# Gating on ScalarE, x sums moved, two sums reordered, and a rearranged last pair in a fused attention and mixture-of-experts kernel

## The chip, the cores and the metric

The kernel runs on one core of a Trainium2 chip. The time is the device time of that core in microseconds (us). A program on one core has no second die to compare with, so a run counts as fast unless it is over 1.5% above the fastest of its kernel.

Short names of the engines: PE is TensorE (matrix products), DVE is VectorE, ACT is ScalarE, POOL is GpSimd, SP is SyncE (here it issues stores). PEld is the loading of TensorE's stationary operand. PSUM is the memory that TensorE writes its products to (the tiles named `ps`), SBUF the memory that holds the other tiles. A name with a q, such as SPq, is an engine's own issue queue.

## The reference, cut to what matters

```python
x = cosformer_attention(q, k, v)          # 4608 tokens x 512; scaled, kept transposed
logits = x @ w_gate                       # 4608 x 8 experts
P = np.exp(logits - logits.max())
for _ in range(8):                        # the routing: rows and columns in turn
    P /= P.sum(1, keepdims=True) + 1e-09
    P /= P.sum(0, keepdims=True) + 1e-09
    P *= N / E
for e in range(8):
    h = np.maximum(x @ w1[e], 0.0)
    out += P[:, e:e + 1] * (h @ w2[e])
```

Every expert runs over all tokens. The output is a sum over experts, each part scaled per token by its column of `P`; this scaling is called the gating.

Of the kernel before, what the change touches and what calls it, by code (L numbers as in the profile page):

```python
# [25 lines left out]
def kernel(  # L26
# [10 lines left out]
    nc = tc.nc  # L37
# [12 lines left out]
    FT = F // P  # L50
    TCH = 512
    NJ = N // TCH
    assert KT == HK and N % TCH == 0

    ctx.enter_context(nc.allow_low_precision("fp16 operands of the matmuls"))
    ctx.enter_context(nc.allow_non_contiguous_dma(reason="256 byte runs and up"))
# [103 lines left out]
            else:  # L160
                ve.tensor_copy(out=acc(g), in_=y_ps)

    def store(g, both=False):
        for half in range(2):
            w_ = 2 * g + half
            b, c = w_ // C, w_ % C
            rows = out[b * S : (b + 1) * S].rearrange("(p c) d -> p c d", c=C)
            (nc.scalar if half and both else nc.sync).dma_start(
                out=rows[:, c, :], in_=acc(g)[half * HP : (half + 1) * HP, :]
            )  # L170

    with ExitStack() as p1:
# [413 lines left out]
                    fn(*args)  # L586


    se = nc.scalar
    ps_k = ctx.enter_context(tc.tile_pool(name="ps_k", bufs=1, space=bass.MemoryType.PSUM))  # L590
    wB = ctx.enter_context(tc.tile_pool(name="wB", bufs=1))
    hB = ctx.enter_context(tc.tile_pool(name="hB", bufs=1))
# [103 lines left out]

    def snapshot(ps, name):
        t = u_pool.tile([P, TU], F16, name=name)
        nc.scalar.copy(out=t[:], in_=ps[:, 0:TU])
        return t  # L700

    late = []
# [1 line left out]
    def group(hT, tw, xs, n, i, fill):  # L704

        b11, T1, b21, b22, T2, T3, T4 = tw
        s1, s2, s4 = (t[:] for t in xs)
        h11, h12 = hT[:, i, 0:TU], hT[:, FH + i, 0:TU]
        h21, h22 = hT[:, i, TU : 2 * TU], hT[:, FH + i, TU : 2 * TU]
        X = ps_h[0].tile([P, TCH], FP32, name="h_ps")  # L710
        product(X, b11, x_part(0, 0, n), True)
        nc.scalar.copy(out=Y[:, 0:TU], in_=X[:, 0:TU])  # L712
        fill()
        for fn in late:
            fn()
        late.clear()
        fill()
        product(X, T2, s2, False)
        u2 = snapshot(X, "u2")
        fill()  # L720
        product(Y, b21, x_part(0, 1, n), False)
        nc.scalar.activation(out=h11, in_=Y[:, 0:TU], func=AF.Relu)  # L722
        fill()
        product(X, T1, s1, False)
        u4 = snapshot(X, "u4")
        fill()
        product(Z, T3, x_part(1, 0, n), True)
        add_relu(h22, Z, u4)
        fill()
        product(X, b22, s4, False)  # L730
        nc.scalar.activation(out=h12, in_=X[:, 0:TU], func=AF.Relu)  # L731
        fill()

        def last():
            product(Z, T4, x_part(1, 1, n), False)
            add_relu(h21, Z, u2)

        late.append(last)


    class Pair:
        def __init__(self, k, hT, e, w, c1, g1, c2, g2, first, last):
            self.last = last
            self.hT, self.e, self.w, self.g1, self.g2, self.first = hT, e, w, g1, g2, first
            self.a11, self.a12 = hT[:, 0:FH, c1 : c1 + P], hT[:, FH:FT, c1 : c1 + P]
            self.a21, self.a22 = hT[:, 0:FH, c2 : c2 + P], hT[:, FH:FT, c2 : c2 + P]
            self.rows = rows2[k % 3][:]
            self.U, self.V = self.rows[:, 0:DH], self.rows[:, DH : 2 * DH]
            self.W = W2[:, k % 2 * DH : (k % 2 + 1) * DH]

        def mult(self, ps, lhs, rhs, start=False):
# [4 lines left out]
                )  # L756

        def add(self, g, rows, a=None):
            a = acc(g) if a is None else a
            ve.scalar_tensor_tensor(  # L760
                out=a, in0=rows, scalar=P_tok[:, g, self.e : self.e + 1], in1=a,
                op0=ALU.mult, op1=ALU.add,
            )

        def sums(self):
            name = "hs_last" if self.last else "hs"
            pool = u_pool if self.last else hs_pool
            S1, S2, S4 = (pool.tile([P, FH, P], F16, name=f"{name}{k_}") for k_ in (1, 2, 4))
            for out_, in0, in1, op in (
                (S1[:], self.a21, self.a22, ALU.add), (S2[:], S1[:], self.a11, ALU.subtract),  # L770
                (self.a21, self.a11, self.a21, ALU.subtract),
                (S4[:], self.a12, S2[:], ALU.subtract),
            ):
                (nc.gpsimd if self.last else ve).tensor_tensor(  # L774
                    out=out_, in0=in0, in1=in1, op=op
                )
            self.S1, self.S2, self.S4 = S1[:], S2[:], S4[:]

        def step(self, name):
# [3 lines left out]
            if name == "P1":  # L783
                if self.first:

                    tw2[0:2] = [t_pool.tile([P, FH, DH], F16, name=f"V{k_}")[:] for k_ in (2, 3)]
                    ve.tensor_tensor(out=tw2[0], in0=b22, in1=b12, op=ALU.subtract)
                    ve.tensor_tensor(out=tw2[1], in0=tw2[0], in1=b11, op=ALU.subtract)
                self.mult(self.U, self.a11, b11, True)
                nc.scalar.copy(out=self.W, in_=self.U)  # L790
                if not self.last:
                    self.sums()
            elif name == "P7":

                if self.first:
                    tw2[2:3] = [t_pool.tile([P, FH, DH], F16, name="V4")[:]]
                    ve.tensor_tensor(out=tw2[2], in0=b21, in1=tw2[0], op=ALU.subtract)
                self.mult(self.V, self.a21, tw2[1])
            elif name == "P6":
                self.mult(self.U, self.S2, tw2[0])  # L800
                self.add(self.g2, self.rows)
            elif name == "P2":
                self.mult(self.W, self.a12, b21)
                self.add(self.g1, self.W, acc(self.g1)[:, 0:DH])
            elif name == "P4":
                self.mult(self.V, self.a22, tw2[2])
                if self.last:
                    self.add(self.g2, self.V, acc(self.g2)[:, 0:DH])
                    store(self.g2, True)
            elif name == "P5":  # L810
                self.mult(self.U, self.S1, b12)
                if self.last:
                    self.add(self.g2, self.U, acc(self.g2)[:, DH:Dm])
                    return
                swapped = self.rows.rearrange("p (h d) -> p h d", h=2)[:, ::-1, :]
                self.add(self.g2, swapped, acc(self.g2).rearrange("p (h d) -> p h d", h=2))
                if self.e == E - 1:
                    store(self.g2)
            elif name == "P3":
                self.mult(self.U, self.S4, b22)  # L820
                self.add(self.g1, self.U, acc(self.g1)[:, DH:Dm])
                if self.e == E - 1:
                    store(self.g1, self.last)

    tw2 = [None] * 3

    def w2_first(w):
        b11, b12 = w[1][:, 0:FH, 0:DH], w[1][:, 0:FH, DH:Dm]
# [65 lines left out]

        return [(n * UG + i, NG // 2 + n * UG + i) for i in range(UG)]

    def gate(n):

        for pair in of_unit(n):
            for g in pair[::-1]:  # L900
                nc.gpsimd.tensor_scalar(  # L901
                    out=acc(g), in0=acc(g), scalar1=P_tok[:, g, 0:1], scalar2=None, op0=ALU.mult,
                )


    balance = sinkhorn()
# [2 lines left out]
    for i in range(FH):  # L909
        tw, tw_steps[3 + i] = w1_steps(w_next, i)  # L910
        tws.append(tw)
    xs_next = x_tiles()
    sums_x = x_sums(0, xs_next)
    for j in range(B - 1, NJ):
        hT = next_h()
        tiles = halves(hT, w0, [(ts * P, j * TCH // P + ts) for ts in range(TCH // P)])
        for slot in range(NS):
# [7 lines left out]
                gates(B - 1, Z[:])  # L925
            if j == B - 1 and slot:
                next(sums_x, None)
            since = (j - B + 1) * NS + slot - 5
            if since == -4:
                balanced(3)  # L930
# [3 lines left out]

    OFFSETS = {"P1": 0, "P2": 3, "P7": 4, "P6": 5, "P4": 8, "P5": 9, "P3": 13}

    OFFSETS_LAST = {"P1": 0, "P7": 4, "P6": 5, "P2": 7, "P5": 8, "P4": 9, "P3": 10}
    stream = []
    slot2 = -2
    n_pairs = 0  # L940

    def add_pairs(hT, e, w, n):
        nonlocal n_pairs
        for i, (g1, g2) in enumerate(of_unit(n)):
            last = e == E - 1 and n == NU - 1 and i == UG - 1
            pair = Pair(n_pairs, hT, e, w, i * P, g1, TU + i * P, g2, n == 0 and i == 0, last)
            for name, offset in (OFFSETS_LAST if last else OFFSETS).items():
                stream.append((7 * n_pairs + offset, pair, name))
            n_pairs += 1
# [13 lines left out]
    def pair_fill():  # L963
        nonlocal k_fill, slot2
        k_fill += 1
        if k_fill % 4 and stream and stream[0][0] <= slot2:
            _, pair, name = stream.pop(0)
            pair.step(name)
        slot2 += bool(k_fill % 4)

    mark(Y[:])
    for e in range(1, E):
        w = w_next
        for n in range(NU):
            hT = next_h()
            xs = xs_next
            for i in range(FH):
                group(hT, tws[i], xs, n, i, start_fill if e == 1 and n == 0 else pair_fill)
                m = (n + 1) % NU
                if e == 1 and m:  # L980

                    if i == 0:
                        xs_next = x_tiles()
                        sums_x = x_sums(m, xs_next)
# [15 lines left out]
            if e == 1 and n == 0:  # L1000
# [4 lines left out]
                    pass  # L1005
                mark(W2[:])
                w2_first(w)
                ve = nc.vector
            if e == 1:
                gate(n)  # L1010
            if n == 0 and e + 1 < E:
                w_next = new_weights(wA if e % 2 else wB)
                load_w1(w_next, e + 1, 1)
# [2 lines left out]
            add_pairs(hT, e, w, n)  # L1016
    for fn in late:
        fn()

    stream[-1][1].sums()  # L1020
    while stream:
        _, pair, name = stream.pop(0)
        pair.step(name)
# [1 line left out]
_INS = ['q', 'k', 'v', 'moe_w_gate', 'moe_w1', 'moe_w2']  # L1025
_OUTS = [((4608, 512), 'float32')]
# [25 lines left out]
```

## The kernel before: the parts that the change touches

Expert 0 is computed plainly while the attention and the routing still run, so its part goes into the accumulator `acc` before `P` is known. It has to be multiplied by `P[:, 0]` later; this is the gating that the change moves. There are 36 tiles `acc(g)` of 128 tokens by 512 columns in fp32.

Experts 1 to 7 use a Strassen-like scheme of seven products in place of eight, which needs sums of blocks of x, of the weights and of h. The tokens of an expert are cut into six units. A unit has four groups of seven products for `h` (each product is two matmuls of 384 columns), and between them stand the steps of "pairs": a pair is two tiles of 128 tokens, with seven products P1 to P7 of four matmuls of 256 columns.

Three engines serve TensorE. In each group ScalarE copies or takes the relu out of PSUM five times. VectorE makes the other relus in one custom instruction that adds a snapshot ("add-and-relu", 0.54 to 0.56 us each in the trace before), makes four sums of halves of h for each pair, and adds the gated products into `acc`.

```python
def group(hT, tw, xs, n, i, fill):        # fill() emits the next step of a pair
    X = ps_h[0].tile([P, TCH], FP32, name="h_ps")
    product(X, b11, x_part(0, 0, n), True)
    nc.scalar.copy(out=Y[:, 0:TU], in_=X[:, 0:TU])     # one such copy per group
    fill()
    # ... the last product of the group before, into Z ...
    fill()
    product(X, T2, s2, False)
    u2 = snapshot(X, "u2")                # the first snapshot, on ScalarE
    fill()
    product(Y, b21, x_part(0, 1, n), False)
    nc.scalar.activation(out=h11, in_=Y[:, 0:TU], func=AF.Relu)
    fill()
    product(X, T1, s1, False)
    u4 = snapshot(X, "u4")                # the second snapshot
    fill()
    product(Z, T3, x_part(1, 0, n), True)
    add_relu(h22, Z, u4)                  # VectorE; frees the bank Z
    fill()
    product(X, b22, s4, False)
    nc.scalar.activation(out=h12, in_=X[:, 0:TU], func=AF.Relu)
    fill()

def sums(self):                           # of one pair; a21 is overwritten by a11 - a21
    # ...
    for out_, in0, in1, op in (
        (S1[:], self.a21, self.a22, ALU.add), (S2[:], S1[:], self.a11, ALU.subtract),
        (self.a21, self.a11, self.a21, ALU.subtract),
        (S4[:], self.a12, S2[:], ALU.subtract),
    ):
        (nc.gpsimd if self.last else ve).tensor_tensor(out=out_, in0=in0, in1=in1, op=op)

def gate(n):                              # in the second expert, once per unit n
    for pair in of_unit(n):
        for g in pair[::-1]:
            nc.gpsimd.tensor_scalar(
                out=acc(g), in0=acc(g), scalar1=P_tok[:, g, 0:1], scalar2=None, op0=ALU.mult,
            )
# ...
stream[-1][1].sums()                      # the last pair's sums, on GpSimd
while stream:                             # the steps of the last pairs, without groups between
    _, pair, name = stream.pop(0)
    pair.step(name)
```

TensorE's instructions are held in written order to the end. ScalarE's are in the attention part, and VectorE's up to the second expert's first unit; after that a scheduler orders them, and may move one ahead of another where nothing depends on the order.

The softmax here doesn't subtract the row's maximum and nothing guards it: scores larger than these inputs give would overflow.

## Time and profile before

The time is 1012.0 us (median of four runs, 1011.84 to 1012.25).

| what | reading | view |
|---|---|---|
| TensorE busy | 983.8 us, 97% of the span | page, part 1 |
| TensorE idle, 200 to 300 us | 6.7 us | windows of 5 us |
| of it waits on VectorE's add-and-relu | 3.5 us in five waits | timeline of TensorE |
| GpSimd's gatings | 36, on average 1.66 and 1.68 us in the two groups | groups by form |
| half rate in the tail | four groups, 0.99 to 1.06 us instead of 0.60 us | timeline |

These lines of the page give the busy time of the engines and, for TensorE, VectorE and GpSimd, the share of each of 40 equal slices in tenths (9 is 90% and more).

```profile
PE 983.8 (97%) x8062; PEld 690.7 (68%) x8062; DVE 840.3 (83%) x1861; ACT 556.5 (55%) x1250; POOL 117.3 (12%) x116
PE   7999999998999999999999999999999999999996
DVE  5888777689999888888879888988789888987876
POOL 6312200009930000000000000000000000000001
```

TensorE is at 9 in every slice but the first, the last and the tenth. In the tenth and eleventh GpSimd is at 9, and VectorE is at 9 as well (56.3 of the 60 us from 228 to 288 us).

The timeline of TensorE between 215 and 280 us, the lines with a mark of idle time (start, duration, engine, line, operation, and in brackets the idle time before it and what ended it):

```profile
219.66 0.20 PE L100 MATMUL copied_ps<-colp,ones_col 128*1 128x8 f32 x2 [1.20 <-DVE colp L100]
224.84 0.20 PE L100 MATMUL copied_ps<-colp,ones_col 128*1 128x8 f32 x2 [0.78 <-DVE colp L100]
...
235.97 0.48 PE L100 MATMUL p_ps<-xT,T_0_3375 128*128 128x384 f16 x2 [0.77 <-DVE H L693]
246.50 0.48 PE L100 MATMUL p_ps<-xT,T_2_3381 128*128 128x384 f16 x2 [1.14 <-DVE H L693]
256.34 0.48 PE L100 MATMUL p_ps<-xT,T_0_3375 128*128 128x384 f16 x2 [0.74 <-DVE H L693]
...
275.79 0.48 PE L100 MATMUL p_ps<-xT,T_0_3375 128*128 128x384 f16 x2 [0.53 <-DVE H L693]
```

The first two waits are for the routing's column sums (`colp`). The others are for the add-and-relu (line 693), which must empty the bank `p_ps` (called Z in the code) before the next product into it.

Why VectorE is late shows in the groups by form between 228 and 288 us (line, engine, operation, shapes, count, then busy us and the mean of one in ns). The first line is GpSimd's gating; the next are VectorE's sums of two fp16 tiles in SBUF, and the last an add that reads PSUM.

```profile
L901 POOL TENSOR_SCALAR acc_lo<-acc_lo,P_tok 128x512 f32<-128x512 f32 x32 | 53.2, 1678 | 16.7 <-DVE P_tok L100 16.6
L774 DVE TENSOR_TENSOR H<-H 128x512 f16<-128x512 f16 x9 | 4.8, 529 | 0.0
L774 DVE TENSOR_TENSOR hs_4203<-hs_4202,H 128x512 f16<-128x512 f16 x1 | 1.2, 1190 | 0.0
L760 DVE SCALAR_TENSOR_TENSOR acc_lo<-rows_ps,P_tok,acc_lo 128x512 f32<-128x512 f32 x16 | 11.8, 740 | 2.6 <-PE rows_ps L100 2.6
```

A sum takes up to 1.19 us there, and 0.42 us between 340 and 400 us, where GpSimd is quiet. The add that reads PSUM takes 0.74 us there and 0.75 us later. So the sums are slow beside GpSimd's gatings and the add that reads PSUM is not; below, such a slowing is called a collision. But not every sum is hit: GpSimd is busy for 59.4 of the 60 us, and 11 of the 36 sums take 0.57 us or more, while 25 keep 0.41 to 0.44 us. What decides which sums are hit is not shown.

The tail, in the timeline, with the same columns:

```profile
989.77 1.21 POOL L774 TENSOR_TENSOR hs_last_13227<-hs_last_13226,H 128x512 f16<-128x512 f16 x1
990.00 1.26 DVE L774 TENSOR_TENSOR hs_13251<-hs_13250,H 128x512 f16<-128x512 f16 x1
991.18 1.37 DVE L774 TENSOR_TENSOR H<-H 128x512 f16<-128x512 f16 x1
...
992.60 0.61 PE L100 MATMUL rows_ps<-V_12078,H 128*128 128x256 f16 x4 [1.98 <-DVE H L774]
...
994.55 0.99 PE L100 MATMUL rows_ps<-w2e,hs_13178 128*128 128x256 f16 x4 [0.90 <-DVE acc_hi L760]
995.34 1.06 PE L100 MATMUL rows_ps<-w2e,H 128*128 128x256 f16 x4
```

GpSimd's sums for the last pair collide with VectorE's for an earlier pair: those of VectorE take up to 1.37 us, and those of GpSimd rise from 1.15 to 1.33 us. TensorE waits 1.98 us for the third of these, `a11 - a21` (written into `H`), then 0.90 us more, and then its matmuls run at about half the rate for a while: four groups last 0.79 to 0.86 us from start to start, where 0.44 us is usual. The granted clock is 0.70 from 995 to 1000 us, 0.96 in the 5 us before and 1.00 from 985 to 990 us.

### The profile page before, as it was taken

How to read it: one execution, taken by the hardware profiler on the slowest of the kernel's cores; microseconds unless marked ns; L12 is line 12 of the kernel's file. 1: busy time of each engine (PE TensorE's matmuls, PEld its weight loads, DVE VectorE, ACT ScalarE, POOL GpSimd, SP SyncE). 2: the span in 40 equal slices, each digit the busy share in tenths (PEclk: the TensorE clock that was granted, in tenths of full speed). 3: DMA queues.
4: the chain of work that ended last, by engine and by line, in shares of the span. 5: the costliest groups of instructions: out<-in, count | busy, mean ns of one | idle time of the engine just before them, and what ended most of it. 6: DMA issues, size and time to landing. Idle time of an engine off the chain costs nothing.

```text
span 1010.2 us, 20651 instructions
## 1 busy us (share of the span) xinstructions
PE 983.8 (97%) x8062; PEld 690.7 (68%) x8062; DVE 840.3 (83%) x1861; ACT 556.5 (55%) x1250; POOL 117.3 (12%) x116
## 2 busy tenths in 40 slices
PE   7999999998999999999999999999999999999996
PEld 6555555445677777777777777777777777777775
DVE  5888777689999888888879888988789888987876
ACT  5766666355555555555555555555555555555551
POOL 6312200009930000000000000000000000000001
PEclk8999999999999999999999999999999999999998
DMA  9966510531302331044013310133103401114434
GB/s 168 201 91 86 88 20 1 107 58 41 81 24 50 64 67 47 25 80 76 25 48 66 65 49 25 36 78 66 49 24 67 89 25 33 39 33 127 113 87 113
DMA packets 51762, 66.50 MB, mean 66 GB/s; under 512 B 4816, under 2 KB 43472, under 8 KB 51664
## 3 DMA queue, kind: packets, MB, share of 16 engines
q0 software_dynamic: 27232, 30.94, 19.8%
q1 hardware_dynamic: 24272, 33.98, 12.4%
q8 instruction: 63, 1.03, 0.4%
q14 instruction: 35, 0.29, 0.1%
q10 hardware_dynamic: 160, 0.26, 0.1%
HBM read 83.12 MB, written 12.98 MB: 95 GB/s over the span
## 4 chain that ended last, share of the span: by engine, by line
PE 88%; DVE 9%; DMA 1%; issue 1%; ACT 1%; POOL 0%; DVEq 0%; POOLq 0%; ACTq 0%
PE rows_ps L100 32%; PE h_ps L100 25%; PE p_ps L100 10%; PE copied_ps L100 10%; PE y_ps L100 5%; PE small_ps L100 4%; DVE H L693 1%; DVE k_p L100 1%; DVE acc_lo L760 1%; DMA k_ld<-in_k_dram 1%; DVE q_pT L100 1%; DVE acc_hi L760 1%; DVE q_p L100 0%; DMA q_ld<-in_q_dram 0%; DVE den L100 0%
## 5 line engine op out<-in xcount | busy, mean ns | idle before, releaser
L760 DVE SCALAR_TENSOR_TENSOR acc_lo<-rows_ps,P_tok,acc_lo 128x512 f32<-128x512 f32 (+1 forms) x322 | 205.0, 640 | 75.1 <-PE rows_ps L100 75.1
L100 PEld LDWEIGHTS <-H 128*128 128x128 f16 x2080 | 203.5, 98 | 85.6 <-DVE H L774 2.3
L100 PEld LDWEIGHTS <-w1e 128*128 128x128 f16 x1632 | 155.8, 98 | 58.3 <-issue 3.6
L100 PE MATMUL h_ps<-xT,w1e 128*128 128x384 f16 (+1 forms) x616 | 152.9, 350 | 0.0
L731 ACT ACTIVATE H<-h_ps 128x384 f16<-128x384 f32 x168 | 82.5, 491 | 112.0 <-PE h_ps L100 112.0
L712 ACT COPY copied_ps<-h_ps 128x384 f32<-128x384 f32 x168 | 78.7, 468 | 41.2 <-PE h_ps L100 40.3
L722 ACT ACTIVATE H<-copied_ps 128x384 f16<-128x384 f32 x168 | 82.7, 492 | 23.5 <-PE copied_ps L100 23.5
L100 PE MATMUL rows_ps<-w2e,H 128*128 128x256 f16 (+1 forms) x568 | 91.7, 286 | 0.0
L100 PE MATMUL copied_ps<-xT,w1e 128*128 128x384 f16 x336 | 82.1, 326 | 0.0
L100 PE MATMUL copied_ps<-w2e,H 128*128 128x256 f16 x504 | 75.6, 273 | 0.0
L118 POOL DMA_DIRECT2D w1e<-in_moe_w_dram x11 | 8.3, 770 | 455.2 <-DVE T_3_10517 L671 83.4
L760 DVE SCALAR_TENSOR_TENSOR acc_lo<-copied_ps,P_tok,acc_lo 128x256 f32<-128x256 f32 x126 | 60.1, 477 | 0.5
L760 DVE SCALAR_TENSOR_TENSOR acc_hi<-rows_ps,P_tok,acc_hi 128x512 f32<-128x512 f32 (+1 forms) x57 | 42.0, 736 | 20.5 <-PE rows_ps L100 20.3
L790 ACT COPY copied_ps<-rows_ps 128x256 f32<-128x256 f32 x126 | 45.0, 357 | 23.3 <-PE rows_ps L100 23.0
L901 POOL TENSOR_SCALAR acc_lo<-acc_lo,P_tok 128x512 f32<-128x512 f32 x32 | 53.2, 1678 | 16.7 <-DVE P_tok L100 16.6
L100 PE MATMUL y_ps<-w2e,hT 128*128 128x512 f16 x224 | 54.7, 380 | 0.0
L774 DVE TENSOR_TENSOR H<-H 128x512 f16<-128x512 f16 x125 | 54.1, 433 | 0.0
L100 ACT ACTIVATE hT<-h_ps 128x512 f16<-128x512 f32 x54 | 32.3, 600 | 17.0 <-PE h_ps L100 16.6
L100 DVE TENSOR_TENSOR xT<-small_ps,rb 128x384 f16<-128x384 f32 x64 | 26.2, 451 | 16.6 <-ACT rb L100 16.5
L100 PEld LDWEIGHTS <-hT 128*128 128x128 f16 x224 | 19.5, 98 | 25.0 <-issue 5.8
L100 ACT COPY rb<-small_ps 128x384 f32<-128x384 f32 x64 | 22.4, 402 | 22.7 <-PE small_ps L100 22.6
L100 DVE TENSOR_SCALAR q_pT<-small_ps 128x384 f16<-128x384 f32 x46 | 25.0, 553 | 9.3 <-PE small_ps L100 8.8
(2450 smaller groups left out, 2036.3 us busy)
## 6 DMA issues: line engine op xcount, KB each, us to landing
out_dram<-acc_lo SPq DMA_DIRECT2D x63, 128.0 KB, 2.4
w1e<-in_moe_w_dram POOLq DMA_DIRECT2D x7, 1024.0 KB, 9.0
w2e<-in_moe_w_dram POOLq DMA_DIRECT2D x7, 1024.0 KB, 9.3
k_ld<-in_k_dram POOLq DMA_DIRECT2D x16, 288.0 KB, 6.3
v_ld<-in_v_dram POOLq DMA_DIRECT2D x16, 288.0 KB, 6.9
q_ld<-in_q_dram POOLq DMA_DIRECT2D x16, 288.0 KB, 6.4
w1e<-in_moe_w_dram POOLq DMA_DIRECT2D x4, 256.0 KB, 10.5
w2e<-in_moe_w_dram POOLq DMA_DIRECT2D x4, 256.0 KB, 10.8
```

What stands on the lines that cost most here:

```text
L100: i = getattr(self.engine, name)(*args, **kwargs)
L118: nc.gpsimd.dma_start(out=w[0][:, :, f0:f1], in_=view[:, :, f0:f1])
L693: latest = ve._custom_dve(TENSOR_ADD_SAT, out=out, in0=ps[:, 0:TU], in1=t[:], s0=FP32_MAX, s1=0.0)
L712: nc.scalar.copy(out=Y[:, 0:TU], in_=X[:, 0:TU])
L722: nc.scalar.activation(out=h11, in_=Y[:, 0:TU], func=AF.Relu)
L731: nc.scalar.activation(out=h12, in_=X[:, 0:TU], func=AF.Relu)
L760: ve.scalar_tensor_tensor(out=a, in0=rows, scalar=P_tok[:, g, self.e : self.e + 1], in1=a, op0=ALU.mult, op1=ALU.add,)
L774: (nc.gpsimd if self.last else ve).tensor_tensor(out=out_, in0=in0, in1=in1, op=op)
L790: nc.scalar.copy(out=self.W, in_=self.U)
L901: nc.gpsimd.tensor_scalar(out=acc(g), in0=acc(g), scalar1=P_tok[:, g, 0:1], scalar2=None, op0=ALU.mult,)
```

## The change

Its intent: take the gating from GpSimd, so that VectorE is not held up, and give it to ScalarE, which is 55% busy; take four sums of x out of the second expert's first unit; and shorten the tail. The diff, cut to its core:

```diff
-            if e == 1:
-                gate(n)                                   # six tiles at once, on GpSimd
+def gate(g, pool=None):
+    if pool is None:
+        se.mul(out=acc(g), in_=acc(g), mul=P_tok[:, g, 0:1])          # ScalarE
+    else: ...                                             # GpSimd, for the first two tiles only
 def pair_fill():
     ...
+        if (k_fill % 7 == 6 or k_fill % 7 == 4 and k_fill % 4 in (1, 2)) and ungated:
+            gate(ungated.pop(0))
+        if e == 2:
+            se = nc.scalar           # ScalarE in written order to the end of the second expert
 # x sums of the second unit, beside the last plain block of expert 0
+            if j == NJ - 1:
+                if slot == 0:
+                    sums_x = x_sums(1, xs_first[1])
+                next(sums_x, None)
 def sums(self, after=None):
-                (S1[:], self.a21, self.a22, ALU.add), (S2[:], S1[:], self.a11, ALU.subtract),
+                (S1[:], self.a21, self.a22, ALU.add),
                 (self.a21, self.a11, self.a21, ALU.subtract),
+                (S2[:], S1[:], self.a11, ALU.subtract),
                 (S4[:], self.a12, S2[:], ALU.subtract),
+                # the last pair's (GpSimd) wait for `after`, VectorE's last sum of the pair before
-    OFFSETS_LAST = {"P1": 0, "P7": 4, "P6": 5, "P2": 7, "P5": 8, "P4": 9, "P3": 10}
+    OFFSETS_LAST = {"P1": 0, "P2": 3, "P7": 4, "P6": 7, "P5": 8, "P4": 9, "P3": 10}
+            if last:
+                self.V = Z[:, 0:DH]                       # the two halves in two banks
 # the last tile is stored in two column halves, the first as soon as P2 is in
+                    store(self.g1, slice(0, DH), both)    # both = (nc.sync, nc.scalar)
+                        store(self.g1, slice(DH, Dm), both)
-    stream[-1][1].sums()
     while stream:
         _, pair, name = stream.pop(0)
         pair.step(name)
+        if pair is final[-2] and name == "P1":
+            final[-1].sums(pair.summed)
```

The second and third of the four sums change places. (`k_fill` counts the calls of `fill()`, and so sets at which steps a gating is emitted.)

More of the change, by code (lines that the diff above doesn't have):

```diff
@@ L52 @@
     NJ = N // TCH
-    assert KT == HK and N % TCH == 0
+    assert NG % 12 == 0 and KT == HK and N % TCH == 0
     ctx.enter_context(nc.allow_low_precision("fp16 operands of the matmuls"))
@@ L161, in ffn2, with store @@
                 ve.tensor_copy(out=acc(g), in_=y_ps)
-    def store(g, both=False):
-        for half in range(2):
+    def store(g, cols=slice(0, Dm), queues=(nc.sync, nc.sync)):
+        for half, queue in enumerate(queues):
             w_ = 2 * g + half
@@ L167, in store @@
             rows = out[b * S : (b + 1) * S].rearrange("(p c) d -> p c d", c=C)
-            (nc.scalar if half and both else nc.sync).dma_start(
-                out=rows[:, c, :], in_=acc(g)[half * HP : (half + 1) * HP, :]
+            queue.dma_start(
+                out=rows[:, c, cols], in_=acc(g)[half * HP : (half + 1) * HP, cols]
             )
@@ L586 @@
                     fn(*args)
-    se = nc.scalar
     ps_k = ctx.enter_context(tc.tile_pool(name="ps_k", bufs=1, space=bass.MemoryType.PSUM))
@@ L698, in snapshot @@
         t = u_pool.tile([P, TU], F16, name=name)
-        nc.scalar.copy(out=t[:], in_=ps[:, 0:TU])
+        se.copy(out=t[:], in_=ps[:, 0:TU])
         return t
@@ L711, in group @@
         product(X, b11, x_part(0, 0, n), True)
-        nc.scalar.copy(out=Y[:, 0:TU], in_=X[:, 0:TU])
+        se.copy(out=Y[:, 0:TU], in_=X[:, 0:TU])
         fill()
@@ L721, in group @@
         product(Y, b21, x_part(0, 1, n), False)
-        nc.scalar.activation(out=h11, in_=Y[:, 0:TU], func=AF.Relu)
+        se.activation(out=h11, in_=Y[:, 0:TU], func=AF.Relu)
         fill()
@@ L730, in group @@
         product(X, b22, s4, False)
-        nc.scalar.activation(out=h12, in_=X[:, 0:TU], func=AF.Relu)
+        se.activation(out=h12, in_=X[:, 0:TU], func=AF.Relu)
         fill()
@@ L758, in add @@
         def add(self, g, rows, a=None):
+            assert g not in ungated
             a = acc(g) if a is None else a
@@ L763, in add, with sums @@
             )
-        def sums(self):
+        def sums(self, after=None):
             name = "hs_last" if self.last else "hs"
@@ L769, in sums @@
             for out_, in0, in1, op in (
-                (S1[:], self.a21, self.a22, ALU.add), (S2[:], S1[:], self.a11, ALU.subtract),
+                (S1[:], self.a21, self.a22, ALU.add),
                 (self.a21, self.a11, self.a21, ALU.subtract),
+                (S2[:], S1[:], self.a11, ALU.subtract),
                 (S4[:], self.a12, S2[:], ALU.subtract),
             ):
-                (nc.gpsimd if self.last else ve).tensor_tensor(
+                i = (nc.gpsimd if self.last else ve).tensor_tensor(
                     out=out_, in0=in0, in1=in1, op=op
                 )
+                if self.last and after is not None:
+                    tc.add_manual_dep(
+                        i.ins,
+                        after.ins.name,
+                        mybir.DependencyInfo(
+                            mybir.DependencyClass.Sync, mybir.DependencyReason.DATA
+                        ),
+                        reason="VectorE's sums first",
+                    )
+                    after = None
+            self.summed = i
             self.S1, self.S2, self.S4 = S1[:], S2[:], S4[:]
@@ L789, in step @@
                 self.mult(self.U, self.a11, b11, True)
-                nc.scalar.copy(out=self.W, in_=self.U)
+                se.copy(out=self.W, in_=self.U)
                 if not self.last:
@@ L797, in step @@
                     ve.tensor_tensor(out=tw2[2], in0=b21, in1=tw2[0], op=ALU.subtract)
-                self.mult(self.V, self.a21, tw2[1])
+                self.mult(self.V, self.a21, tw2[1], self.last)
             elif name == "P6":
                 self.mult(self.U, self.S2, tw2[0])
-                self.add(self.g2, self.rows)
+                if self.last:
+                    self.add(self.g2, self.U, acc(self.g2)[:, 0:DH])
+                    self.add(self.g2, self.V, acc(self.g2)[:, DH:Dm])
+                else:
+                    self.add(self.g2, self.rows)
             elif name == "P2":
@@ L804, in step @@
                 self.add(self.g1, self.W, acc(self.g1)[:, 0:DH])
+                if self.last:
+                    store(self.g1, slice(0, DH), both)
             elif name == "P4":
@@ L808, in step @@
                     self.add(self.g2, self.V, acc(self.g2)[:, 0:DH])
-                    store(self.g2, True)
+                    store(self.g2, queues=both)
             elif name == "P5":
@@ L822, in step @@
                 if self.e == E - 1:
-                    store(self.g1, self.last)
+                    if self.last:
+                        store(self.g1, slice(DH, Dm), both)
+                    else:
+                        store(self.g1)
     tw2 = [None] * 3
+    both = (nc.sync, nc.scalar)
     def w2_first(w):
@@ L895, in of_unit @@
         return [(n * UG + i, NG // 2 + n * UG + i) for i in range(UG)]
-    def gate(n):
-        for pair in of_unit(n):
-            for g in pair[::-1]:
-                nc.gpsimd.tensor_scalar(
-                    out=acc(g), in0=acc(g), scalar1=P_tok[:, g, 0:1], scalar2=None, op0=ALU.mult,
-                )
+    def gate(g, pool=None):
+        if pool is None:
+            se.mul(out=acc(g), in_=acc(g), mul=P_tok[:, g, 0:1])
+        else:
+            pool.tensor_scalar(
+                out=acc(g), in0=acc(g), scalar1=P_tok[:, g, 0:1], scalar2=None, op0=ALU.mult,
+            )
+    ungated = [g for n in range(NU) for pair in of_unit(n) for g in pair]
     balance = sinkhorn()
@@ L911 @@
         tws.append(tw)
-    xs_next = x_tiles()
+    xs_first = [x_tiles() for _ in range(2)]
+    xs_next = xs_first[0]
     sums_x = x_sums(0, xs_next)
@@ L935 @@
     OFFSETS = {"P1": 0, "P2": 3, "P7": 4, "P6": 5, "P4": 8, "P5": 9, "P3": 13}
-    OFFSETS_LAST = {"P1": 0, "P7": 4, "P6": 5, "P2": 7, "P5": 8, "P4": 9, "P3": 10}
+    OFFSETS_LAST = {"P1": 0, "P2": 3, "P7": 4, "P6": 7, "P5": 8, "P4": 9, "P3": 10}
     stream = []
+    final = []
     slot2 = -2
@@ L946, in add_pairs @@
             pair = Pair(n_pairs, hT, e, w, i * P, g1, TU + i * P, g2, n == 0 and i == 0, last)
+            if e == E - 1 and n == NU - 1:
+                final.append(pair)
             for name, offset in (OFFSETS_LAST if last else OFFSETS).items():
@@ L980 @@
                 if e == 1 and m:
+                    if n == 0:
+                        xs_next = xs_first[1]
+                        continue
                     if i == 0:
@@ L1007 @@
                 w2_first(w)
+                for _ in range(2):
+                    gate(ungated.pop(0), nc.gpsimd)
                 ve = nc.vector
-            if e == 1:
-                gate(n)
             if n == 0 and e + 1 < E:
```

## The prediction

The gains of 2.9, 3.8 and 0.4 us come to 7.1 us, which takes 1012.0 us to 1004.9, given as 1005.0 us.

> **What bounds the kernel.** TensorE: busy 97%, and 88% of the chain that ended last. So the change can win back only TensorE's idle or slow time. By windows of 5 us, TensorE idles 6.7 us between 200 and 300 us, almost never from 300 to 980.
>
> The 6.7 us, from the idle marks of the timeline: 2.0 us waiting for the routing's column sums on VectorE (219.7 and 224.8 us); 1.2 us on ScalarE copies (213 to 234 us); 3.5 us in five waits on VectorE's add-and-relu (236 to 276 us). There GpSimd runs 36 gatings, 1.66 us each (226 to 288 us), and VectorE is 100% busy. Its fp16 additions (128x512) take 0.8 to 1.2 us when they collide, against 0.42 us later. [...] the adds that read PSUM keep 0.74 us.
>
> In the tail GpSimd's four sums (988.5 to 993.6 us) collide with another pair's sums on VectorE (up to 1.37 us instead of 0.42). TensorE idles 2.0 + 0.9 us, then runs four groups at half rate (1.06 instead of 0.60 us). After 990.46 us, 20 steps of 0.437 us could end at 999.4; they end at 1006.0.
>
> **What changes.** TensorE's order changes only in the last pair.
> - 34 gatings move to ScalarE, an estimated 0.70 us each (from a 128x512 activation's 0.60 us and a 128x576 one from SBUF, 0.67), 24 us in all; ScalarE, 55% busy, rises to about 80%. Most fit the idle 0.66 us before the relu that waits for TensorE. Those before the second snapshot have only 0.2 to 0.3 us: 1 to 2 us of stall in all. The scheduler hoists the last four to about 232 us, where two stand before a snapshot: 1 to 1.5 us of stall.
> - Four x sums (0.55 us each) move from 215–231 us to VectorE's gaps near 201–206 us: most of the 2.0 us returns.
> - VectorE's 3.5 us of waits nearly vanish: without GpSimd it needs about 96% of TensorE's time.
>
> Middle: idle falls from 6.7 to about 3.8 us. Gain 2.9 us.
> - Tail: GpSimd starts after VectorE's sums, whose four take 1.6 us instead of 4.4, and the half rate should go. But VectorE's remaining work (11.4 us) is longer than TensorE's 9, and GpSimd's chain of four (about 1 us each, from 995.5) may hold the last pair 0.5 to 1 us. Two banks remove one of two waits of 0.57 us. Gain about 3.8 us. The last store is half as large: 0.4 us.
>
> **Prediction: 1005.0 us, range 1001.5 to 1008.5.** Faster by over 2%: 1%; within 2%: 98%; slower: 1%.
>
> **What would show it.** Fp16 sums at 0.42 us and no TensorE wait on add-and-relu from 240 to 290 us; gatings of 0.70 us on ScalarE; TensorE waits on snapshots of 2 to 3 us between 230 and 320 us; sums from 989 to 997 us at 0.42 us; no half-rate matmuls; a wait for GpSimd's last sums.
>
> **What would make it wrong.** Gatings delay snapshots more, so that stalls only change owner (1008); the tail still idles over 2 us before the last pair [...] (1007); or the gatings fit everywhere and the tail is nearly gapless (1001).

## The result, and the profile after

The kernel after takes 1003.08 us (median of four runs, 1002.52 to 1004.44), the kernel before 1012.01 us. The ratio of the fast runs is 0.9914, with an interval of 0.9896 to 0.9931: within 2%, and 8.9 us faster. A ratio is the mean time of one kernel's fast runs over that of the other's of the same rounds, so it is not quite the ratio of the medians.

The page of the kernel after, the busy time:

```profile
PE 981.3 (98%) x8062; PEld 689.3 (69%) x8062; DVE 829.2 (83%) x1862; ACT 574.7 (57%) x1284; POOL 60.3 (6%) x82
```

The timeline of TensorE shows only these marks over 0.3 us between 215 and 300 us:

```profile
219.13 0.19 PE L100 MATMUL copied_ps<-colp,ones_col 128*1 128x8 f32 x2 [1.20 <-DVE colp L100]
224.31 0.20 PE L100 MATMUL copied_ps<-colp,ones_col 128*1 128x8 f32 x2 [0.78 <-DVE colp L100]
```

All five waits on the add-and-relu are gone, and both waits on the column sums are there to the hundredth. The groups by form, VectorE's sums between 228 and 288 us, and ScalarE's gatings:

```profile
L777 DVE TENSOR_TENSOR H<-H 128x512 f16<-128x512 f16 x9 | 3.8, 419 | 0.1
L100 ACT ACTIVATE acc_lo<-acc_lo,P_tok 128x512 f32<-128x512 f32 x28 | 20.4, 727 | 0.0
```

The sums are back at 0.42 us. A gating takes 0.73 us, 4% more than the 0.70 us that the prediction estimated from two ScalarE activations in the trace before (128x512 in 0.60 us, and 128x576 from SBUF in 0.67 us).

The tail, in the timeline:

```profile
984.11 0.43 DVE L777 TENSOR_TENSOR H<-H 128x512 f16<-128x512 f16 x1
984.45 0.42 DVE L777 TENSOR_TENSOR hs_13244<-hs_13243,H 128x512 f16<-128x512 f16 x1
...
991.95 0.33 PEld L100 LDWEIGHTS <-H 128*128 128x128 f16 x4 [0.23 <-POOL H L777]
993.06 0.33 PEld L100 LDWEIGHTS <-hs_last_13295 128*128 128x128 f16 x4 [0.34 <-POOL hs_last_13295 L777]
994.25 0.60 PE L100 MATMUL rows_ps<-w2e,hs_last_13294 128*128 128x256 f16 x4 [0.58 <-DVE acc_hi L762]
```

VectorE's sums take 0.42 us, and no group of matmuls runs at half rate. Two weight loads wait for GpSimd's chain of sums, by 0.23 and 0.34 us. The first load of a group usually starts 0.10 us ahead of its products (988.61 and 988.71 us) and here 0.01 us (991.95 and 991.96 us), so the two groups of products start later by less: 0.55 and 0.66 us after the group before, where 0.44 us is usual.

### Where the time came from

TensorE's order of instructions is the same in both kernels up to the last pair, so the same instruction can be looked up in both and the times compared. ScalarE's copy of X to Y is a handy landmark: there is one in each of the 168 groups. The first, the 30th (in the third expert's second unit) and the 168th, from the timeline of ScalarE, before:

```profile
209.60 0.46 ACT L712 COPY copied_ps<-h_ps 128x384 f32<-128x384 f32 x1
349.40 0.46 ACT L712 COPY copied_ps<-h_ps 128x384 f32<-128x384 f32 x1 [0.33 <-PE h_ps L100]
983.33 0.46 ACT L712 COPY copied_ps<-h_ps 128x384 f32<-128x384 f32 x1 [0.33 <-PE h_ps L100]
```

and after:

```profile
209.07 0.46 ACT L100 COPY copied_ps<-h_ps 128x384 f32<-128x384 f32 x1
345.85 0.46 ACT L711 COPY copied_ps<-h_ps 128x384 f32<-128x384 f32 x1 [0.33 <-PE h_ps L100]
977.59 0.46 ACT L711 COPY copied_ps<-h_ps 128x384 f32<-128x384 f32 x1 [0.33 <-PE h_ps L100]
```

They cut the span into pieces: the start (to the first copy), the middle (first to 30th), the steady part (30th to 168th), the tail (to the start of the last four matmuls, from the timeline), and the end (to the end of the span). The two spans are 1010.2 and 1000.8 us.

| piece | before | after | gain |
|---|---|---|---|
| start | 209.60 | 209.07 | 0.53 |
| middle | 139.80 | 136.78 | 3.02 |
| steady | 633.93 | 631.74 | 2.19 |
| tail | 22.04 | 17.84 | 4.20 |
| end | 4.83 | 5.37 | -0.54 |

The start varies from 208.33 to 211.20 us over the twelve profiles (the kernels before and after and ten variants), and the end from 4.47 to 5.37 us, with no pattern that follows an edit. So these two pieces are read as noise, and they are most of the scatter of the times. The middle and the tail repeat to about 0.1 us where an edit doesn't touch them, the steady part to 0.3 us (see below). These three pieces are what the experiments are judged by.

The gain of 2.19 us in the steady part was in no term of the prediction. By the spacing of the landmarks it lies in six steps of 0.33 us, one near the start of each expert from the third on, and in one of 0.28 us at the 109th group. The latter, a gap without a mark in TensorE's products, is absent from every variant with the gating on ScalarE and present in the two that keep it on GpSimd; why is not known. The timeline at the first of the six, before:

```profile
348.62 0.42 DVE L774 TENSOR_TENSOR hs_5236<-H,hs_5235 128x512 f16<-128x512 f16 x1
348.95 0.55 DVE L693 CUSTOM_DVE_ANT_0 H<-p_ps,u_5246 128x384 f16<-128x384 f32 x1
...
349.56 0.48 PE L100 MATMUL p_ps<-xT,T_0_4845 128*128 128x384 f16 x2 [0.25 <-DVE H L693]
```

and after:

```profile
345.07 0.55 DVE L692 CUSTOM_DVE_ANT_0 H<-p_ps,u_5246 128x384 f16<-128x384 f32 x1
345.54 0.41 DVE L777 TENSOR_TENSOR hs_5236<-H,hs_5235 128x512 f16<-128x512 f16 x1
345.67 0.49 PE L100 MATMUL p_ps<-xT,T_0_4843 128*128 128x384 f16 x2
```

Before, the pair's fourth sum (`hs_5236`) stands ahead of the add-and-relu, and TensorE waits 0.25 us for the bank. There are six such waits of 0.25 us before, and none after. After, the scheduler has the two the other way round, and there is no wait. Whether the reordered sums did this, or the gating, the trace alone cannot tell.

### The profile page after: what moved, and what is told of

Read it like the earlier page. It is cut to its first block, busy times and chain, and to the rows that moved or that the text cites. A ratio compares the mean times of both kernels' runs of the same rounds, so it can differ in the third digit from the quotient of the medians.

```text
span 1000.8 us, 20629 instructions
## 1 busy us (share of the span) xinstructions
PE 981.3 (98%) x8062; PEld 689.3 (69%) x8062; DVE 829.2 (83%) x1862; ACT 574.7 (57%) x1284; POOL 60.3 (6%) x82
## 4 chain that ended last, share of the span: by engine, by line
PE 72%; issue 21%; DVE 4%; ACT 1%; DMA 1%; POOL 1%; POOLq 0%; ACTq 0%; DVEq 0%
PE rows_ps L100 25%; PE h_ps L100 21%; PE copied_ps L100 8%; PE p_ps L100 8%; PE y_ps L100 5%; PE small_ps L100 5%; DVE k_p L100 1%; DMA v_ld<-in_v_dram 1%; DVE q_pT L100 1%; DVE q_p L100 0%; DVE den L100 0%; DVE xT L100 0%; DVE acc_lo L100 0%; DVE P_tok L100 0%; DVE v_aug_240 L100 0%
## 5 line engine op out<-in xcount | busy, mean ns | idle before, releaser
L730 ACT ACTIVATE H<-h_ps 128x384 f16<-128x384 f32 x144 | 70.6, 490 | 95.1 <-PE h_ps L100 95.1
L711 ACT COPY copied_ps<-h_ps 128x384 f32<-128x384 f32 x144 | 67.5, 469 | 35.3 <-PE h_ps L100 35.3
L721 ACT ACTIVATE H<-copied_ps 128x384 f16<-128x384 f32 x144 | 70.8, 492 | 20.4 <-PE copied_ps L100 20.4
L804 ACT COPY copied_ps<-rows_ps 128x256 f32<-128x256 f32 x111 | 39.7, 357 | 17.6 <-PE rows_ps L100 17.6
L100 ACT ACTIVATE H<-h_ps 128x384 f16<-128x384 f32 (+1 forms) x40 | 21.3, 532 | 15.4 <-PE h_ps L100 14.7
```

What stands on the lines that cost most here:

```text
L100: i = getattr(self.engine, name)(*args, **kwargs)
L711: se.copy(out=Y[:, 0:TU], in_=X[:, 0:TU])
L721: se.activation(out=h11, in_=Y[:, 0:TU], func=AF.Relu)
L730: se.activation(out=h12, in_=X[:, 0:TU], func=AF.Relu)
L804: se.copy(out=self.W, in_=self.U)
```

## The experiments

Theory A, formed after the result: the change works by three separate mechanisms. GpSimd's gating held VectorE's sums up; the new order of the four sums lets the scheduler put the add-and-relu earlier; and the tail gains from uncollided sums. Its rivals are that one of these did it all, and that the steps of the prediction which do not show in the trace (x sums, ScalarE's stalls) are nonetheless there.

First a check of the edits. The traces show the following, apart from a few missing records. Moving the gating alone leaves VectorE's order as before; reordering the sums alone gives VectorE the order of the kernel after from the second expert on, but for the x sums and the last adds of the last pair. So the scheduler's rearrangement comes from the reordered sums.

All results, with the pieces from one profile each:

| variant | time, us | middle | steady | tail |
|---|---|---|---|---|
| kernel before | 1012.0 | 139.80 | 633.93 | 22.04 |
| kernel after | 1003.08 | 136.78 | 631.74 | 17.84 |
| before + reordered sums | 1006.70 | 137.94 | 632.02 | 20.28 |
| before + gating on ScalarE | 1009.16 | 137.24 | 633.70 | 21.85 |
| after, gating on GpSimd | 1005.05 | 137.95 | 632.03 | 17.85 |
| after, x sums back | 1003.11 | 136.89 | 631.75 | 17.85 |
| after, old order of the sums | 1005.01 | 136.87 | 633.67 | 18.06 |
| after, last sums not held | 1005.99 | 136.78 | 631.73 | 19.84 |
| after, one bank, old last steps | 1004.34 | 136.78 | 631.74 | 19.28 |
| after, last tile stored whole | 1003.24 | 136.78 | 631.68 | 17.84 |
| gatings moved | 1001.91 | 135.70 | 631.67 | 17.84 |
| and slack for the routing | 1001.44 | 135.19 | 631.95 | 17.84 |

All variants gave correct results, and each time is the median of four fast runs. The kernel before, run beside them, gave medians of 1011.89 to 1012.05 us. The kernel after was not run beside them, so small differences from it are read from the pieces.

### The reordered sums alone

```diff
 # on the kernel before
-                (S1[:], self.a21, self.a22, ALU.add), (S2[:], S1[:], self.a11, ALU.subtract),
+                (S1[:], self.a21, self.a22, ALU.add),
                 (self.a21, self.a11, self.a21, ALU.subtract),
+                (S2[:], S1[:], self.a11, ALU.subtract),
```

> The kernel before with one edit: the second and third of the four half sums of a pair change places (a11-a21 is made second). VectorE's written order is then that of the kernel after except for the x sums. Theory A (the reorder lets the scheduler put the fourth sum behind the add-and-relu): TensorE's six waits of 0.25 us on add-and-relu, one at the start of each expert from the third on, are gone, and the pace between 330 and 975 us gains about 2.2 us against before; in the tail the wait of 2.0 us for a11-a21 shrinks by about 1.3 us; time 1008.5 to 1010. Rival (the gating or the x sums moved VectorE's order): the six waits stay, time 1012.

Measured: 1006.70 us, ratio 0.9954 (0.9939 to 0.9969). That is 5.3 us, more than half of the whole gain, for two lines in another order. The six waits are gone: the steady part is 632.02 us, 1.91 us shorter. The tail is 1.76 us shorter: the longest wait there is now 0.69 us, and the half rate is gone, although GpSimd's sums are not held back there. But the middle is shorter too, by 1.86 us, which was not expected and took the time below the stated 1008.5: although GpSimd still gates, TensorE's waits on the add-and-relu there shrink from 3.5 to 1.5 us. Its timeline still shows them:

```profile
236.86 0.48 PE L100 MATMUL p_ps<-xT,T 128*128 128x384 f16 x2 [0.43 <-DVE H L692]
255.55 0.48 PE L100 MATMUL p_ps<-xT,T 128*128 128x384 f16 x2 [0.37 <-DVE H L692]
```

So where the scheduler puts a sum against the add-and-relu matters even while GpSimd gates.

### The gating alone, and the gating undone

The first variant is the kernel before with the gating of the kernel after, the second the kernel after with the gating of the kernel before:

```diff
 # on the kernel before
-            if e == 1:
-                gate(n)
+        if (k_fill % 7 == 6 or k_fill % 7 == 4 and k_fill % 4 in (1, 2)) and ungated:
+            gate(ungated.pop(0))          # se.mul
 # on the kernel after: the same lines the other way
```

In the first of these expectations the words that name a mechanism for theory A are cut. Theory A is the one above: GpSimd's gating held VectorE's sums up.

> The kernel before with the gating alone moved to ScalarE (two of 36 left on GpSimd); VectorE's order is exactly that of before. Theory A [...]: the five waits on add-and-relu between 236 and 276 us, 3.5 us, are gone and the gain is about 3 us, 1009; the six waits of 0.25 us at each expert's start stay. Rival (the reorder or the x sums brought the middle gain): 1012.

> The kernel after with the gating back on GpSimd, unit by unit. Theory A: the time rises by about 3 us to 1006, VectorE's fp16 sums in 230 to 290 us take 0.8 us and more again, and TensorE waits on add-and-relu there. Rival (x sums and reorder suffice): 1003 to 1004.

Measured: 1009.16 us (ratio 0.9975, 0.9960 to 0.9991) and 1005.05 us. With the gating alone the middle is 2.56 us shorter, VectorE's order is unchanged, and its sums in this stretch take 0.41 to 0.43 us. So this gain comes from taking the gatings off GpSimd. One wait on the add-and-relu is left, at the start of the second unit:

```profile
235.72 0.48 PE L100 MATMUL p_ps<-xT,T 128*128 128x384 f16 x2 [0.29 <-DVE H L692]
```

In the second variant the middle is 1.17 us longer (137.95 against 136.78), not 3. The expectation of 1006 us was too high. The gating and the reorder remove the same waits, so they overlap: 2.56 and 1.86 us alone, 3.02 us in the kernel after with the x sums included. What each is worth depends on which is done first.

### The x sums

```diff
 # on the kernel after
-            if j == NJ - 1:
-                if slot == 0:
-                    sums_x = x_sums(1, xs_first[1])
-                next(sums_x, None)
 # and in the second expert the sums of the next unit are made from its first unit on, as before
```

> The kernel after with the second unit's x sums back beside the second expert's first unit. The prediction's step (these sums delay the routing's column sums): TensorE's two waits on column sums grow from 2.0 us and the time rises by 1 to 2 us, to 1004.5. Rival (they ran in VectorE's idle time there, the chain of the routing is bound elsewhere): waits of 1.20 and 0.78 us as in both kernels, time unchanged within 0.4 us.

Measured: 1003.11 us, the same time; the middle is 136.89 us, 0.11 us longer. Both waits on the column sums are 1.20 and 0.78 us, exactly as in the kernels before and after. The prediction's step is refuted. These sums ran while VectorE waited for TensorE's broadcast: in the kernel after VectorE stands idle for 0.77 us at the place where the kernel before had one of them, and the chain from the broadcast to the column sum is as long as it was (2.29 us from start to start, 2.28 us before). At their new place the sums do lie in the way: in the kernel after, the product of the broadcast at 206.28 us waits 0.16 us for VectorE, and the two column sums around it are 4.87 us apart, against 4.64 us before and 4.65 us in this variant. This loss of 0.22 us lies in the start piece, whose own scatter hides it. So the move won nothing.

### The old order of the sums, in the kernel after

The edit is that of the first experiment the other way round.

> The kernel after with the four half sums in their old order. Theory A (the order decides where the scheduler puts the fourth sum against the add-and-relu at each expert's start): six waits of 0.25 us return, the pace from 330 to 975 us loses about 2 us, the tail some 0.4 us; time 1005.5. Rival (once GpSimd is quiet VectorE has room and the order is worth nothing): 1003.1.

Measured: 1005.01 us (ratio 0.9934, 0.9919 to 0.9948). The steady part is 1.93 us longer, so the six waits are due to the order of the sums, shown now from both sides. The middle is only 0.09 us longer: there the rival is right, and once GpSimd is quiet the order is worth nothing. The tail loses 0.22 us, and its half rate stays away; so either of the two, the new order or the held sums, is enough to remove it.

### The tail: last sums, banks, stores

```diff
 # last sums not held, on the kernel after
+    final[-1].sums()
     while stream:
         _, pair, name = stream.pop(0)
         pair.step(name)
-        if pair is final[-2] and name == "P1":
-            final[-1].sums(pair.summed)
 # one bank and the old order of the last steps, on the kernel after
-            if last:
-                self.V = Z[:, 0:DH]
-    OFFSETS_LAST = {"P1": 0, "P2": 3, "P7": 4, "P6": 7, "P5": 8, "P4": 9, "P3": 10}
+    OFFSETS_LAST = {"P1": 0, "P7": 4, "P6": 5, "P2": 7, "P5": 8, "P4": 9, "P3": 10}
 # last tile stored whole, on the kernel after
-                    store(self.g1, slice(0, DH), both)
-                        store(self.g1, slice(DH, Dm), both)
+                    store(self.g1, queues=both)
```

> The kernel after with GpSimd's four last sums issued ahead of the closing loop, not held behind VectorE's. Theory A: they collide with VectorE's sums of the third pair from the end, which take up to 1.37 us; TensorE waits about 0.7 us each for a11-a21 and the second sum, as in the run with the reorder alone; the half-rate stretch does not come back, [...]; time about 1.4 us longer, 1004.5. Rival (the reorder has already taken the whole gain of the tail): 1003.1.

Measured: 1005.99 us; the tail is 2.00 us longer, against the 1.4 us expected. The timeline shows the collision and the waits that were foreseen, and no half rate:

```profile
986.38 1.26 DVE L777 TENSOR_TENSOR H<-H 128x512 f16<-128x512 f16 x1
987.69 0.61 PE L100 MATMUL rows_ps<-V,H 128*128 128x256 f16 x4 [0.69 <-DVE H L777]
988.98 0.61 PE L100 MATMUL rows_ps<-V,hs 128*128 128x256 f16 x4 [0.68 <-DVE hs L777]
...
991.33 0.60 PE L100 MATMUL rows_ps<-V,H 128*128 128x256 f16 x4 [0.65 <-DVE acc_hi L762]
```

By the starts of the products, each of the first two waits costs 0.85 us, because matmul records overlap (0.60 us long, 0.44 us from start to start), and the third, 0.65 instead of 0.35 us, adds 0.30 us. The expectation counted the marks of the first two alone. The matmuls keep their 0.60 and 0.61 us after these waits of 0.69, 0.68 and 0.65 us, where in the kernel before they slowed after waits of 1.98 and 0.90 us. How much waiting it takes is not shown.

> The kernel after with both halves of the last pair's second row in one bank and the old order of the last pair's steps. Theory A: two waits of 0.58 us on VectorE between the last three products instead of one, the last product starts 0.3 to 0.6 us later, time 1003.5. Rival: GpSimd's chain of sums sets the end, no change.

Measured: 1004.34 us; the tail is 1.44 us longer, more than twice the expected size. Two waits of 0.58 and 0.57 us stand before the last two products, as expected, but there are two more:

```profile
991.22 0.61 PE L100 MATMUL rows_ps<-V,H 128*128 128x256 f16 x4 [0.38 <-POOL H L775]
992.33 0.61 PE L100 MATMUL rows_ps<-V,hs_last 128*128 128x256 f16 x4 [0.50 <-POOL hs_last L775]
```

With the old order of the steps P7 and P6 come earlier and meet GpSimd's chain of four sums (1.15 us each in the kernel after). The new order puts P2 ahead of both, and another pair's P3 ahead of P6. The variant undoes both edits at once, so how the 1.44 us divide between banks and order was not measured.

> The kernel after with the last tile stored whole at the end, on both queues. The prediction's step: the last store is twice as large, the end comes 0.4 us later. Rival (SyncE's queue of store issues, 0.55 us each, is the limit and has one issue less to do): the last store is issued 0.3 us sooner on SyncE, and the end is the same or up to 0.3 us sooner.

Measured: 1003.24 us, tail 17.84 us, end 4.99 us. The end is 4.47 to 5.37 us in the profiles whose last store is a half tile and 4.83 to 4.99 us in those (this variant, the kernel before and the two variants of it) whose last store is a whole one. So halving the last store gained nothing that shows above this scatter. The rival's reason was not shown either: the last store was issued 0.3 us sooner in this variant, but equally so in other variants with the halved store. Two such issues in a row took 1.10 us at their shortest on SyncE in the kernel after, 0.55 us each.

### What ScalarE's gatings cost, and a faster version

The prediction expected stalls where a gating stands before the second snapshot, but TensorE's timeline shows no idle marks there from 234 us on. Looking closer, this is the kernel after; the fourth line's product into `h_ps` has to wait for that snapshot (`u_3941`):

```profile
241.13 0.71 ACT L100 ACTIVATE acc_lo<-acc_lo,P_tok 128x512 f32<-128x512 f32 x1
241.74 0.49 PE L100 MATMUL p_ps<-xT,T_2_3380 128*128 128x384 f16 x2
241.74 0.47 ACT L100 CAST u_3941<-h_ps 128x384 f16<-128x384 f32 x1
242.26 0.48 PE L100 MATMUL h_ps<-S_3390,w1e 128*128 128x384 f16 x2
```

After a product of this size the next starts 0.32 us later; here it is 0.52 us, without a mark. A record is 0.48 us long, so it overlaps the next by 0.16 us, and that much of a delay leaves no idle time in the trace. The variant moves these two gatings per unit to the place ahead of the first snapshot, where ScalarE idles for 0.57 us:

```diff
 # on the kernel after
-        if (k_fill % 7 == 6 or k_fill % 7 == 4 and k_fill % 4 in (1, 2)) and ungated:
+        if (k_fill % 7 == 6 or k_fill % 7 == 2 and k_fill % 4 in (0, 1)) and ungated:
 # and the stores of the last two pairs alternate between both queues
```

> The kernel after with the two gatings per unit that stand before the second snapshot of a group moved ahead of the first one, where ScalarE idles 0.57 us, and with the stores of the last two pairs on both queues. Theory A (each gating before the second snapshot delays TensorE by 0.1 to 0.2 us, too short for an idle mark): the stretch from the second expert's start to its end, 136.78 us in the kernel after, falls by 0.4 us to 136.4. Rival (ScalarE's gatings cost nothing): 136.78 again. The time falls by 0.4 us at most, to 1002.7, within the noise of the start.

Measured: 1001.91 us (1001.72 to 1002.34), ratio 0.9903 to the kernel before; the middle falls by 1.08 us to 135.70. The same two products now:

```profile
243.21 0.49 PE L100 MATMUL p_ps<-xT,T 128*128 128x384 f16 x2
243.54 0.49 PE L100 MATMUL h_ps<-S,w1e 128*128 128x384 f16 x2
```

The gain lies in six groups, 0.16 to 0.20 us each. So the stall that the prediction named is there, within its 1 to 2 us, and was hidden because it is made of short gaps that carry no mark. It is not all gone: another product per unit still starts 0.46 to 0.49 us after the one before it (0.46 to 0.61 us in the kernel after).

The last variant adds slack to the routing's chain:

```diff
 # on the variant above
-        if k_fill % 6 != 1:
+        if k_fill % 6:                     # the column sum's product one slot later
             balanced(1)
-            if g % 2 == 0:
+            if g % 2 == 0 or g >= NG - TCH // P:      # the last block's copies on ScalarE
                 se.copy(out=acc(g), in_=y_ps)
```

> The run before with two more edits in the second expert's first unit: the product that sums the columns comes one slot later (VectorE's chain gets a slot more), and the last block's outputs are copied by ScalarE alone, which takes one copy of 0.69 us out of that chain. Theory A (TensorE's 2.0 us of waits are set by VectorE's chain from one broadcast to the next column sums): the two waits of 1.20 and 0.78 us fall to less than half, the stretch to 135.4 us or less, time 1001.5. Rival (the chain is as long as TensorE's work of an iteration, so that a later product only moves the wait to the next broadcast): stretch above 136.2.

Measured: 1001.44 us (1001.10 to 1002.16), ratio 0.9899 (0.9884 to 0.9914). Here are the marks of TensorE's timeline in the second expert's first unit:

```profile
219.11 0.48 PE L100 MATMUL h_ps<-S,w1e 128*128 128x384 f16 x2 [0.40 <-ACT u L100]
224.37 0.20 PE L100 MATMUL copied_ps<-colp,ones_col 128*1 128x8 f32 x2 [0.45 <-DVE colp L100]
229.92 0.48 PE L100 MATMUL h_ps<-S,w1e 128*128 128x384 f16 x2 [0.73 <-ACT u L100]
```

The waits on column sums fall from 1.98 to 0.45 us, but one wait on ScalarE's snapshots, 0.40 us, comes in, and another grows from 0.24 to 0.73 us, because the copies moved to ScalarE, 0.59 us each, stand ahead of them (one at 218.09 us, the snapshot after it at 218.57 us). The middle gains 0.51 us and is 135.19 us, within the 135.4 us that theory A stated, although much of the 1.5 us taken from the waits on column sums is lost to the others. This version is faster than the kernel before, clear of noise. It is 1.6 us below the kernel after by the medians, but they ran in different rounds, and the intervals of their ratios overlap. What supports the gain is the profile: the middle is 1.59 us shorter, and the steady part 0.21 us longer.

## Why the prediction was right or wrong

The time was right: 1005.0 us predicted, 1003.08 us measured, within 1001.5 to 1008.5. The forecast gains add up to 7.1 us, against 8.9 us measured. That the sum came so close is partly luck, as the steps show:

- **VectorE's 3.5 us of waits "nearly vanish": right.** They are gone, the sums are back at 0.42 us (VectorE is busy for 47.1 us and TensorE for 51.8 us from 236 to 288 us, 91% and not the 96% of the forecast), and the gating alone gives 2.56 us in the middle with VectorE's order unchanged. TensorE did not get all of the 3.5 us: one wait of 0.29 us was left with the gating alone, and the gatings' own stalls, below, took part of it back.
- **"Most of the 2.0 us returns" by moving the x sums: wrong.** Both waits stayed to the hundredth of a us, and moving the sums back cost 0.11 us there and saved 0.22 us in the start. The sums stood in VectorE's idle time, while it waited for TensorE's broadcast. I took work near a wait for work ahead of it in the chain.
- **ScalarE's gatings: 0.70 us each predicted, 0.73 measured. Stalls before the second snapshot, "1 to 2 us": right, 1.08 us of it by the variant that moves them.** But the prediction said that they would show as waits on snapshots, and they show no marks.
- **The four hoisted gatings, "1 to 1.5 us of stall": wrong.** The three waits on ScalarE near 230 us are 0.24, 0.28 and 0.30 us, the same in the kernels before and after.
- **Middle, 2.9 us: 3.02 us measured, right by two errors that cancel** (2.0 us not returned, 1 to 1.5 us not lost).
- **Tail, 3.8 us: 4.20 us measured.** The half rate went, and one wait of 0.58 us is left of two. GpSimd's chain of sums delays the last pair's loads by 0.23 and 0.34 us and its products by 0.11 and 0.22 us (0.5 to 1 us predicted). Holding GpSimd's sums back, on which the forecast was built, is worth 2.00 us in the kernel after; not foreseen was that the reorder alone already removes the half rate and 1.76 us.
- **The halved last store, 0.4 us: not seen.** The end's own scatter is 0.9 us.
- **Missed altogether: the reordered sums.** The diff has them in plain sight, and the order of VectorE's instructions showed the rearrangement through the whole kernel. I read it as a matter of the tail. Alone it brings 5.3 us. Of this, 1.9 us lie in the steady part, where the prediction had no gain at all, and these are most of the difference between the predicted and the measured gain.

Left open: which of VectorE's sums GpSimd slows and why, what makes the granted clock fall to 0.70 in the tail before, how banks and step order share 1.44 us in the tail, what makes the one gap of 0.28 us in the steady part, and what makes the start vary by up to 2.9 us between profiles.

## What to carry to other kernels

When one engine serves several consumers in turn, first ask which of its results the limiting engine waits for, and move independent work behind that result; here the order of two sums, made alone, brought 5.3 us, and moving 34 instructions to another engine, made alone, about 2.9 us. Before expecting time back from work moved out of a stretch, check whether it stood in a chain or in the engine's idle time. And TensorE's marks of idle time left out delays of 0.16 to 0.20 us here, six of which made up 1.08 us: compare the starts of the same instruction in two traces to see what they add up to.
